# A delta-rule attention kernel: the first pair's blocks inverted in halves of 16 tokens, and the first loads dealt out over three queues

## The chip, the cores and the metric

The kernel runs on one core of a Trainium2 chip. The metric is the device time of one execution in microseconds (us), as a median of several runs. Beside it stands a profile: one execution recorded by the hardware, whose span runs from the first to the last instruction. Engines are named as in the profile: PE is TensorE (PEld its weight loads), DVE is VectorE, ACT is ScalarE, POOL is GpSimd, SP is SyncE, which here only issues transfers.

## What is computed

A delta-rule attention over 4 batch elements, 8 heads, 768 tokens and a head size of 48, and then a feed-forward block with a cosine gate.

```python
k_n = k / (np.linalg.norm(k, axis=-1, keepdims=True) + 1e-06)
state = np.zeros((B, H, D, D))
for t in range(S):
    kt, vt, bt = (k_n[:, :, t], v[:, :, t], beta[:, :, t, None])
    y[:, :, t] = np.einsum('bhd,bhde->bhe', q[:, :, t], state)
    v_old = np.einsum('bhde,bhd->bhe', state, kt)
    state = state + bt[:, :, :, None] * np.einsum('bhd,bhe->bhde', kt, vt - v_old)
# x is y as (3072, 384): batch and token by head and dimension
h = x @ w_in             # 384 -> 2048
out = (h * np.cos(h)) @ w_out    # 2048 -> 384
```

The kernel doesn't go token by token. It takes a unit of 32 tokens (of all 4 batch elements and 8 heads, 128 rows by 8 heads) at a time, 24 units, two of which form a pair. Within a unit the tokens depend on each other through a triangular 32x32 matrix for each head and batch element, one plus the scaled Gram matrix of the keys above the diagonal. That matrix is inverted, and the inverse is multiplied with the right side (the values less what the state already holds): this is called the solve. The state is then updated once for the unit. The feed-forward block works on pairs: eight hidden steps (products with w_in, then the gate) and an output (products with w_out).

The weights arrive as 64-bit floats and are turned into 32-bit ones on the chip, in 12 blocks of w_in and 16 of w_out, each by ACT, DVE and POOL one after the other.

## The kernel before

A small scheduler in the kernel file orders the work: every task is added with an engine, a cost, the tasks it depends on and a due time, and the instructions are written in the order that a simulation of the engines gives. Its constants are numbers found by tuning; they set the order and nothing else. Each engine then runs its own list strictly in order.

The loads at the start (each tensor of a unit is four transfers, one for each batch element):

```python
load(0, "k")                                   # on SP
near = 130 + C
for cols in (slice(0, near), slice(near, consts_np.shape[1])):
    nc.gpsimd.dma_start(out=consts[:, cols], in_=consts_dr.ap()[:, cols])
load(0, "q", nc.scalar)
for b in range(B):
    nc.gpsimd.dma_start(out=bq[...], in_=beta[b])
load(1, "q")                                   # on SP
load(1, "k", nc.gpsimd)
```

The Gram matrix of a unit is scaled by DVE into g (gram_keys) and written to DRAM (gram_put). Once both units of a pair are there, it is read back with one matrix to each partition row, the same to two partitions (gram_get), and inverted column by column. Each of the two partitions holds every second row of the inverse:

```python
def gram_get(m):
    g_dr = gbs[m]
    gbs[m] = work.tile([128, C, C], FP, name="gb", bufs=GBS)
    for a in range(SPLIT):                     # SPLIT = 2
        nc.sync.dma_start(out=gbs[m][half(a)]..., in_=g_dr...)

def invert(m, tag, columns):
    a, z = gbs[m], zs[m]
    eng = nc.gpsimd if tag is None else nc.vector
    for j in columns:                          # 0 .. C - 2, C = 32
        rows = j // SPLIT + 1
        shape = [128, rows, C - 1 - j]
        ...
        eng.tensor_tensor(                     # L583
            out=part,
            in0=z[:, 0:rows, j, None].to_broadcast(shape),
            in1=a[:, j, None, j + 1 :].to_broadcast(shape),
            op=ALU.mult,
        )
        behind = z[:, 0:rows, j + 1 :]
        eng.tensor_tensor(out=behind, in0=behind, in1=part, op=ALU.subtract)   # L590
```

Pair 0 is inverted by DVE, with z in PSUM (named p_i), and copied to SBUF by ACT (invert_out, L594). All later pairs are inverted by POOL with z in SBUF. The inverse goes to DRAM in one transfer (put, L599) and comes back with four transfers for each unit (get, L608), in the layout that the solve needs:

```python
def get(n):
    zts[n] = work.tile([128, H, C], FP, name="zt")
    z_dr = z_drs[n // 2].rearrange("r s u h b i -> u b (r s) h i")[n % 2]
    for b in range(B):
        nc.sync.dma_start(out=zts[n][quarter(b)], in_=z_dr[b])

def solve(n):
    zt, rhs = zts.pop(n), rhss.pop(n)
    p_u = p_us[n] = bank("one", [128, H, D], "p_u")
    for h in range(H):
        for b in range(B):                     # 32 products of 32x32 by 32x48; L652
            nc.tensor.matmul(p_u[quarter(b), h], zt[quarter(b), h], rhs[quarter(b), h])
```

A unit then goes: solve_out (u, DVE, L660), update (p_s, PE, L673), update_out (st, DVE), within (p_kq, PE, L690), within_out (y, ACT, L701), features (p_z, PE), features_out (x_ffn, ACT, L715), and its columns of x are ready. The first four hidden steps of pair 0 (L728) need only unit 0, the other four unit 1; step k of each four needs the first 3(k+1) blocks of w_in. Later pairs' hidden steps are L745, the outputs L792 and L850. Tiles of g have two buffers, those of u two.

Of the kernel before, what the change touches and what calls it, by code (L numbers as in the profile page):

```python
# [11 lines left out]
FP = mybir.dt.float32  # L12
# [5 lines left out]
C = 32  # L18
# [7 lines left out]
def _consts():  # L26

    p = np.arange(128)
    share = p // 64
    row = SPLIT * np.arange(C // SPLIT)[None, :] + share[:, None]
    return np.concatenate(
        [
            np.eye(128),
            p[:, None] % C < np.arange(C)[None, :],
            p[:, None] // C % 2 == np.arange(2)[None, :],  # L40
            (row[:, :, None] == np.arange(C)).reshape(128, -1),
        ],
        axis=1,
    ).astype(np.float32)


class Order:
# [9 lines left out]
    WINDOW = 133.06  # L57
    LAG = {"PE": 0.2, "DVE": 0.15, "ACT": 0.15, "POOL": 0.2, "SP": 2.0}
    IN_FLIGHT = 8
    STICK = 4.36  # L60
    CHANGE = 0.15
    SMALL = ("gram", "state", "solve", "update", "within")
# [4 lines left out]
        "turn": 16, "gram": 128, "state": 256, "solve": 128, "update": 64, "within": 128,  # L67
# [44 lines left out]
    def run(self, wrote):  # L112
# [8 lines left out]
        for key in ends:  # L121
            engine, cost, due, *_, moves = self.tasks[key]
            for d in self.tasks[key][4]:
# [3 lines left out]
                if left[d] == 0:  # L127
                    ends.append(d)
        for count, (key, task) in enumerate(self.tasks.items()):
# [97 lines left out]
def kernel(  # L227
# [44 lines left out]
    GBS, ZS = 2, 2  # L272
    GATES = 9
# [67 lines left out]
    near = 130 + C  # L341
    for cols in (slice(0, near), slice(near, consts_np.shape[1])):
        nc.gpsimd.dma_start(out=consts[:, cols], in_=consts_dr.ap()[:, cols])
# [3 lines left out]
    eye = consts[:, 130 + C :].rearrange("p (r i) -> p r i", i=C)  # L347
# [3 lines left out]
    for b in range(B):  # L351
        nc.gpsimd.dma_start(
            out=bq[C * b : C * b + H].rearrange("p n t -> p (n t)"), in_=beta[b]
        )
    load(1, "q")
    load(1, "k", nc.gpsimd)
# [165 lines left out]
    def gram_keys(n):  # L522
        g = gs[n] = work.tile([128, H, C], FP, name="g")
# [17 lines left out]
    def gram_put(n):  # L541
        m = n // 2
        if m not in gbs:
            gbs[m] = dram.tile([2, H, B, C, C], FP, name="g_dr")
        nc.sync.dma_start(
            out=gbs[m][n % 2].rearrange("h b j i -> (b j) h i"), in_=gs.pop(n)
        )

    def gram_get(m):

        g_dr = gbs[m]
        gbs[m] = work.tile([128, C, C], FP, name="gb", bufs=GBS)
        for a in range(SPLIT):
            nc.sync.dma_start(
                out=gbs[m][half(a)].rearrange("p j i -> p (j i)"),
                in_=g_dr.rearrange("u h b j i -> (u h b) (j i)"),
# [8 lines left out]

    def invert(m, tag, columns):

# [4 lines left out]
        eng = nc.gpsimd if tag is None else nc.vector  # L572
        for j in columns:
            rows = j // SPLIT + 1
            shape = [128, rows, C - 1 - j]
            if tag is None:
                part = work.tile([128, ROWS * C // 2], FP, name="part")
            else:
                part = ffn_pool.tile([128, ROWS * C // 2], FP, name="part_v", tag="o")
            part = part[:, 0 : shape[1] * shape[2]].rearrange(  # L580
                "p (r i) -> p r i", i=shape[2]
            )
            eng.tensor_tensor(  # L583
                out=part,
                in0=z[:, 0:rows, j, None].to_broadcast(shape),
                in1=a[:, j, None, j + 1 :].to_broadcast(shape),
                op=ALU.mult,
            )
            behind = z[:, 0:rows, j + 1 :]
# [13 lines left out]
    def get(n):  # L603

        zts[n] = work.tile([128, H, C], FP, name="zt")
        z_dr = z_drs[n // 2].rearrange("r s u h b i -> u b (r s) h i")[n % 2]
        for b in range(B):
            nc.sync.dma_start(out=zts[n][quarter(b)], in_=z_dr[b])  # L608
# [38 lines left out]
    def solve(n):  # L647
        zt, rhs = zts.pop(n), rhss.pop(n)
        p_u = p_us[n] = bank("one", [128, H, D], "p_u")
        for h in range(H):  # L650
            for b in range(B):
                nc.tensor.matmul(  # L652
                    p_u[quarter(b), h], zt[quarter(b), h], rhs[quarter(b), h]
                )

    def solve_out(n):

        u = us[n] = work.tile([128, H, 2, D], FP, name="u")
# [250 lines left out]
    def store(p, i, cols=slice(0, DM)):  # L909
# [10 lines left out]
            tt=LEAD + 1, g_gram=2, g_dr=3, gb=GBS, z=ZS, z_dr=3, zt=2, rhs=2, u=2, y=2,  # L920
            x=2, turns=2, r=2, g=GATES, o=2, o_out=2,
        ),
        free={"SP": 5.5, "ACT": 5.6, "POOL": 6.2, "DVE": 6.0, "PE": 6.0},
# [3 lines left out]
    W_IN, W_OUT, LOADS = 62.2, 33.46, -16.83  # L927
    PLAIN = range(1)
    outs_done = [None]
    START = 67.36  # L930
# [314 lines left out]
```

## Time and profile before

| what | us |
|---|---|
| time, median of 3 runs | 702.89 (701.24 to 702.93) |
| span of the profiled execution | 699.6 |
| PE busy | 639.3 (91%) |
| DVE busy | 402.9 (58%) |
| ACT busy | 283.2 (40%) |
| POOL busy | 342.5 (49%) |
| first matmul of a hidden step (p_h, L728) | at 68.45 |
| longest waits: POOL for gb from DRAM, over the whole run | 167.0, in 9 waits |

Times inside the profile count from the start of the span. A row of the groups has the line and engine, the operation, what is written and read, the count, then busy time and mean nanoseconds of one, then idle time of that engine just before it and what ended it. A row of the stretches (one row for each piece of the span that was asked for) has each engine's busy time with its number of instructions. "issue" in a chain of waits is time in which an engine waited for nothing that the profile shows. SPq, ACTq and POOLq are the engines' sequencers; a DMA instruction there is the issue of a transfer and not its duration. The time of an instruction on POOL is rough.

### The profile page before, as it was taken

The numbers are of one execution on the slowest core, as the hardware profiler recorded it, in microseconds if no ns is written. First come the engines' busy times: TensorE is split into PE (matmuls) and PEld (weight loads), VectorE is DVE, ScalarE is ACT, GpSimd is POOL, SyncE is SP. The second block draws the span as 40 slices with busy tenths as digits, with TensorE's granted clock in tenths as the row PEclk, the third lists the DMA queues.
The fourth block names the chain that finished last, engine by engine and source line by source line (L and its number), as shares of the span: only waits on it lengthen the run. The fifth ranks groups of instructions, "written<-read, shape, count | busy, mean of one in ns | idle before, by whom it ended". The sixth has DMA issues, their size and how long they took to land.

```text
span 699.6 us, 25291 instructions
## 1 busy us (share of the span) xinstructions
PE 639.3 (91%) x11096; PEld 568.9 (81%) x11096; DVE 402.9 (58%) x804; ACT 283.2 (40%) x482; POOL 342.5 (49%) x738
## 2 busy tenths in 40 slices
PE   3305799999999999999999999999999999999997
PEld 2205697777898988998998988998998988988997
DVE  4895778876655545556556555556456455444542
ACT  3424467652443542532533532532532532433430
POOL 5469678878508607708607707708508508500000
PEclk9999999999999999999999999999999999999999
DMA  9888656562323133133133133132122120110000
GB/s 174 195 173 181 131 144 162 131 121 38 63 54 72 28 73 72 27 74 70 30 72 72 29 70 72 30 73 48 22 57 49 22 58 26 22 22 14 1 23 22
DMA packets 162833, 49.27 MB, mean 70 GB/s; under 512 B 154212, under 2 KB 157428, under 8 KB 162724
## 3 DMA queue, kind: packets, MB, share of 16 engines
q1 hardware_dynamic: 161252, 46.82, 32.6%
q8 instruction: 87, 1.43, 0.9%
q0 software_dynamic: 384, 0.64, 0.4%
q10 hardware_dynamic: 1088, 0.20, 0.1%
q14 instruction: 22, 0.18, 0.1%
HBM read 36.62 MB, written 11.01 MB: 68 GB/s over the span
## 4 chain that ended last, share of the span: by engine, by line
PE 86%; DMA 5%; DVE 4%; issue 1%; ACT 1%; SPq 1%; ACTq 0%; POOL 0%; DVEq 0%
PE p_h L745 32%; PE p_out L850 29%; PE p_kq L625 4%; PE p_h L728 4%; PE p_s L673 3%; PE p_kq L690 3%; PE p_out L792 3%; PE p_u L652 3%; PE p_g L514 2%; PE p_t L496 2%; PE p_o L850 1%; SPq L330 1%; DVE p_i L590 1%; DVE part_v L583 1%; DMA kp<-in_k_dram 1%
## 5 line engine op out<-in xcount | busy, mean ns | idle before, releaser
L745 PE MATMUL p_h<-x_ffn,w_in 128*128 128x256 f32 x1056 | 241.7, 381 | 1.3 <-DVE g_ffn L782 1.3
L583 POOL TENSOR_TENSOR part<-z,gb 128x126 f32<-128x126 f32 (+22 forms) x341 | 131.2, 385 | 218.4 <-DMA gb<-g_dr 167.0
L745 PEld LDWEIGHTS p_h<-x_ffn,w_in 128*128 128x128 f32 x1056 | 197.1, 190 | 26.8 <-PE p_kq L625 1.0
L590 POOL TENSOR_TENSOR z<-z,part 128x126 f32<-128x126 f32 (+22 forms) x341 | 137.1, 402 | 26.7
L762 DVE SCALAR_TENSOR_TENSOR r<-p_h,turns 128x512 f32<-128x512 f32 x96 | 66.1, 689 | 114.9 <-ACT turns L758 113.7
L850 PE MATMUL p_out<-w_out,g_ffn 128*128 128x192 f32 x672 | 126.0, 333 | 0.8
L758 ACT ACTIVATE turns<-p_h 128x512 int32<-128x512 f32 x96 | 57.1, 594 | 167.6 <-PE p_h L745 154.2
L850 PEld LDWEIGHTS p_out<-w_out,g_ffn 128*128 128x128 f32 x672 | 108.7, 190 | 6.2 <-ACT o L887 3.0
L782 DVE TENSOR_TENSOR g_ffn<-r,p_h 128x512 f32<-128x512 f32 x96 | 65.5, 683 | 53.0 <-ACT r L770 52.7
L850 PE MATMUL p_out<-w_sum,g_ffn 128*128 128x192 f32 x496 | 89.7, 329 | 0.2 <-DVE o L900 0.2
L866 DVE TENSOR_TENSOR g_ffn<-g_ffn 128x256 f32<-128x256 f32 x176 | 79.2, 471 | 15.0 <-PE p_out L850 13.0
L769 ACT ACTIVATE r<-r 128x512 f32<-128x512 f32 x96 | 60.7, 632 | 62.0 <-DVE r L762 61.9
L850 PEld LDWEIGHTS p_out<-w_sum,g_ffn 128*128 128x128 f32 x496 | 81.7, 190 | 2.3 <-DVE o L900 0.4
L770 ACT ACTIVATE r<-r,halfpi 128x512 f32<-128x512 f32 x96 | 69.3, 722 | 3.1
L496 PE MATMUL p_t<-consts,kp 128*128 128x128 f32 x96 | 16.8, 305 | 41.2 <-DMA vp<-in_v_dram 29.6
L900 DVE SCALAR_TENSOR_TENSOR o<-p_out,o 128x192 f32<-128x192 f32 x74 | 25.4, 356 | 48.5 <-PE p_out L850 48.2
L496 PEld LDWEIGHTS p_t<-consts,kp 128*128 128x128 f32 x96 | 13.0, 157 | 43.8 <-issue 38.1
L701 ACT COPY y<-p_kq 128x384 f32<-128x384 f32 x24 | 11.5, 479 | 69.5 <-PE p_kq L690 69.5
L455 POOL TENSOR_TENSOR knrm<-ksum,halves 128x16 f32<-128x16 f32 (+1 forms) x14 | 36.5, 2613 | 5.9 <-DVE ksum L443 3.3
L625 PEld LDWEIGHTS p_kq<-st,kq_t 48*32 48x32 f32 x2944 | 29.4, 107 | 7.1 <-issue 7.0
L625 PE MATMUL p_kq<-st,kq_t 48*32 48x48 f32 x2944 | 32.8, 216 | 1.6 <-issue 1.6
L502 ACT COPY kq_t<-p_t 128x512 f32<-128x512 f32 x48 | 25.7, 588 | 15.9 <-PE p_t L496 15.9
(73 smaller groups left out, 619.8 us busy)
## 6 DMA issues: line engine op xcount, KB each, us to landing
pairs<-in_moe_w_in_dram SPq DMA_DIRECT2D x12, 512.0 KB
gb<-g_dr SPq DMA_DIRECT2D x24, 256.0 KB
pairs<-in_moe_w_out_dram SPq DMA_DIRECT2D x16, 384.0 KB
vp<-in_v_dram SPq DMA_DIRECT2D x96, 48.0 KB
kp<-in_k_dram SPq DMA_DIRECT2D x92, 48.0 KB
qp<-in_q_dram SPq DMA_DIRECT2D x92, 48.0 KB
out_dram<-o SPq DMA_DIRECT2D x23, 192.0 KB
g_dr<-g SPq DMA_DIRECT2D x24, 128.0 KB
```

Of the source, the lines that this page charges most:

```text
L496: nc.tensor.transpose(p_t[:, a, j], src[:, 2 * j : 2 * j + 2], ident)
L583: eng.tensor_tensor(out=part, in0=z[:, 0:rows, j, None].to_broadcast(shape), in1=a[:, j, None, j + 1 :].to_broadcast(shape), op=ALU.mult,)
L590: eng.tensor_tensor(out=behind, in0=behind, in1=part, op=ALU.subtract)
L625: nc.tensor.matmul(p_kq[quarter(b), par, a, j], kq_t[rows48(par), a, j, quarter(b)], st[rows48(par), b // 2, j, b % 2], start=(j == 0 and ...
L745: nc.tensor.matmul(p_h[:, i], w_in[:, t, (f + i) * 128 : (f + i + 1) * 128], xts[p][:, t], start=(t == 0), stop=(t == KT - 1),)
L758: nc.scalar.activation(turns[p, f], p_hs[p, f], AF.Copy, scale=TURN)
L762: nc.vector.scalar_tensor_tensor(out=r, in0=p_hs[p, f], scalar=TURN, in1=turns.pop((p, f)), op0=ALU.mult, op1=ALU.subtract,)
L769: nc.scalar.activation(r, r, AF.Abs)
L770: nc.scalar.activation(r, r, AF.Sin, bias=halfpi, scale=-2.0 * math.pi)
L782: nc.vector.tensor_tensor(out=out, in0=rests.pop((p, f)), in1=p_hs.pop((p, f)), op=ALU.mult,)
L850: nc.tensor.matmul(p_o, left(p, e // 2, a)[:, e % 2], right(e, b), start=(e == 0), stop=(e == FT // 2 - 1), skip_group_check=True,)
L866: nc.vector.tensor_tensor(out=left(p, k, to), in0=left(p, k, one), in1=left(p, k, two), op=op)
```

## The change

Three things are done at once, and the schedule's constants are set anew.

First, pair 0's matrices are inverted in halves of 16 tokens. Only the two 16x16 blocks on the diagonal are inverted, both in the same instructions (the access pattern gets one more dimension of two, from a block to the next), which leaves 15 columns. The 16x16 block between them is not inverted. It is used in the solve instead, for units 0 and 1: solve with the two small inverses, keep the first half's rows (half_out), multiply them with the Gram matrix (cross), take this from the right side of the second half (cross_out), and solve again. For this the tile g must stay in SBUF up to the cross product, so it has four buffers; u has one.

Second, the loads at the start. Unit 1's keys move from the POOL queue to SP, ahead of unit 1's queries. The second part of the constants (the unit matrix that z starts from) comes after beta.

Third, the two transfers of pair 0's gram_get are dealt to SP and ACT, and so are those of get for units 0 and 1.

The meaning is to have the first unit's result, and with it the first hidden step, earlier.

```diff
-    WINDOW = 133.06
+    WINDOW = 74.02
-    STICK = 4.36
+    STICK = 3.35
...
+    HALVED = range(1)
+    GRAMS = 4
...
-    for cols in (slice(0, near), slice(near, consts_np.shape[1])):
-        nc.gpsimd.dma_start(out=consts[:, cols], in_=consts_dr.ap()[:, cols])
+    nc.gpsimd.dma_start(out=consts[:, :near], in_=consts_dr.ap()[:, :near])
...
+    nc.gpsimd.dma_start(out=consts[:, near:], in_=consts_dr.ap()[:, near:])
+    load(1, "k")
     load(1, "q")
-    load(1, "k", nc.gpsimd)
...
+    def twice(ap, step):
+        dims = list(ap.ap)
+        return bass.AP(tensor=ap.tensor, offset=ap.offset, ap=dims[:1] + [(step, 2)] + dims[1:])
...
+        n = C // 2 if m in HALVED else C
         for j in columns:
             rows = j // SPLIT + 1
-            shape = [128, rows, C - 1 - j]
+            shape = [128, rows, n - 1 - j]
+            if n < C:
+                shape = [128, 2] + shape[1:]
...
+            column = z[:, 0:rows, j, None].to_broadcast([128, rows, n - 1 - j])
+            row = a[:, j, None, j + 1 : n].to_broadcast([128, rows, n - 1 - j])
+            behind = z[:, 0:rows, j + 1 : n]
...
+                column = twice(column, (ROWS // 2) * C + n)
+                row = twice(row, n * C + n)
+                behind = twice(behind, (ROWS // 2) * C + n)
+            eng.tensor_tensor(out=part, in0=column, in1=row, op=ALU.mult)
             eng.tensor_tensor(out=behind, in0=behind, in1=part, op=ALU.subtract)
...
+    def solve_half(n):
+        p_us[n] = bank("one", [128, H, D], "p_u")
+        quarters(p_us[n], zts[n], rhss[n])
+    def half_out(n):
+        v = us[n] = work.tile([128, H, D], FP, name="y")
+        nc.scalar.activation(v, p_us.pop(n), AF.Copy, scale=first_half)
+    def cross(n):
+        p_us[n] = bank("one", [128, H, D], "p_u")
+        quarters(p_us[n], gs.pop(n), us.pop(n))
+    def cross_out(n):
+        rhs = work.tile([128, H, D], FP, name="rhs")
+        nc.vector.scalar_tensor_tensor(
+            out=rhs, in0=p_us.pop(n), scalar=less_second, in1=rhss[n],
+            op0=ALU.mult, op1=ALU.add,
+        )
+        rhss[n] = rhs
...
-        u = us[n] = work.tile([128, H, 2, D], FP, name="u")
+        u = us[n] = work.tile([128, H, 2, D], FP, name="u", bufs=1)
...
-    W_IN, W_OUT, LOADS = 62.2, 33.46, -16.83
+    W_IN, W_OUT, LOADS = 57.76, 55.7, 4.07
-    START = 67.36
-    FIRST, STEP = 3.98, 5.5
+    START = 40.69
+    FIRST, STEP = 3.12, 5.9
...
+        if m == 0:
+            add(("gram_get", m), "SP", 0.6, lambda: gram_get(m, range(1)), puts, ...)
+            add(("gram_get2", m), "ACT", 0.6, lambda: gram_get(m, range(1, 2), nc.scalar), puts, ...)
...
+        if n < 2:
+            add(("get", n), "SP", 0.95, lambda: get(n, range(2)), [("put", m)], ...)
+            add(("get2", n), "ACT", 0.95, lambda: get(n, range(2, 4), nc.scalar), [("put", m)], ...)
...
-    add(("beta",), "DVE", 1.3, spread_beta)
+    there = []
+    for key, time in (
+        (("k", 0), 6.6), (("q", 0), 0.3), (("k", 1), 0.8), (("beta_there",), 0.9), (("q", 1), 0.6),
+    ):
+        add(key, "FIRST", time, lambda: None, there, due=0.0)
+        there = [key]
+    add(("beta",), "DVE", 1.3, spread_beta, [("beta_there",)])
```

START, FIRST and STEP set the due times of the hidden steps; W_IN, W_OUT and LOADS those of the weights' additions and loads; WINDOW how far ahead of the most urgent task an engine may go; STICK how long TensorE stays with tasks of one kind. The last part of the diff tells the schedule's simulation when the first loads are there; it emits nothing.

## The prediction

> **What bounds the kernel now.** I read the page's strip of 40 slices first, because this kernel has two regimes and an average over both says nothing. Its first row is TensorE, one digit for 17.5 us.
>
> ```profile
> PE   3305799999999999999999999999999999999997
> ...
> DMA  9888656562323133133133133132122120110000
> ```
>
> From the sixth slice on, TensorE is 9 of 10 in every slice; before that it is mostly idle. While it idles, the DMA row stands at 8 to 9. So the steady part is bound by TensorE and the start by something else. I then cut the span at the events that end each part of the start (the inversion's first and last VectorE instruction, the first solve, the first matmul of pair 0's hidden layer). Columns: stretch, its length, busy time and instructions of PE, PEld, DVE, ACT and POOL, granted clock, DMA share, GB/s.
>
> ```profile
> 0.00:29.36 29.36, 12.41 (x288) 10.11 (x288) 16.44 (x50) 12.58 (x23) 17.87 (x22) 1.00 0.91 187
> 29.36:47.47 18.11, 0.00 (x0) 0.00 (x0) 15.99 (x62) 4.95 (x8) 6.06 (x19) 1.00 0.80 170
> 47.47:58.90 11.43, 1.94 (x8) 1.57 (x9) 8.55 (x12) 2.15 (x4) 10.10 (x18) 1.00 0.78 163
> 58.90:68.45 9.55, 7.54 (x291) 6.46 (x292) 4.45 (x6) 4.69 (x10) 8.61 (x14) 1.00 0.90 211
> 68.45:97.00 28.55, 23.29 (x594) 21.52 (x590) 20.15 (x31) 14.78 (x29) 21.24 (x27) 0.94 0.67 141
> ```
>
> In the first 97 us TensorE works 45.2 us, so 51.8 us are lost there: 46.6 before the hidden layer starts at 68.45, 5.3 between 68.45 and 97. After 116.6 us, by the same view, it works 575.2 of 583.0. What the change can win must come from the start; in the rest only TensorE work counts.
>
> Next, the chain of waits over the start (start, us, what):
>
> ```profile
> 7.23 5.33 DMA kp<-in_k_dram
> ...
> 18.98 4.61 DMA g_dr<-g
> 23.61 0.55 SPq L554
> 24.21 5.06 DMA gb<-g_dr
> 29.59 0.21 DVE p_i L590
> ...
> 47.56 0.59 ACT z L594
> 48.17 0.39 SPq L599
> 48.61 3.39 SPq L330
> ```
>
> Keys, Gram matrix, a trip through DRAM, then 18.1 us in which one VectorE chain is alone on the path, then another trip through DRAM. On the way back the SP queue first issues other loads, with 3.39 us in one of them, before it comes to the inverse. Last, the groups by shape inside the inversion (mean ns is the third number from the end of a row's middle part):
>
> ```profile
> L590 DVE TENSOR_TENSOR p_i<-p_i,part_v 128x136 f32<-128x136 f32 x1 | 0.3, 307 | 0.0
> L583 DVE TENSOR_TENSOR part_v<-p_i,gb 128x136 f32<-128x136 f32 x1 | 0.3, 299 | 0.0
> ...
> L590 DVE TENSOR_TENSOR p_i<-p_i,part_v 128x16 f32<-128x16 f32 x1 | 0.2, 183 | 0.0
> L583 DVE TENSOR_TENSOR part_v<-p_i,gb 128x16 f32<-128x16 f32 x1 | 0.2, 175 | 0.0
> ```
>
> Eight and a half times the elements cost only 124 ns more. The number of instructions is what the inversion pays for.
>
> [...] 1.03 ns per element, and a fixed part of 158 to 166 ns. [...] the engines are busy 0.91 in the first 29 us, while four loads of one tensor take SP 1.8 to 1.9 us to issue. So I count issue time and no bandwidth. [...] In the trace the 64 small matmuls of a solve take 2.00 us at 58.93, after a pause, and 0.88 us at 75.24. I take those durations; the granted clock shown for that stretch is 1.00, so the trace shows the slowness and not its cause.
>
> **The change, part by part.**
>
> *Inversion.* Removed: 31 columns of two VectorE instructions. Left: 15 columns, each doing both 16-token halves in one instruction. From the rows above a column costs 158 + 166 + 2 x 1.03 ns per element, plus two gaps; 62 instructions sum to 16.0 us busy in 18.1 us, so a gap is 34 ns. A column is thus 392 ns + 2.06 ns per element. The old columns have 2856 elements: 31 x 0.392 + 5.88 = 18.0 us, against 18.11 measured, so the formula holds. The new ones have 744: 15 x 0.392 + 1.53 = 7.4 us. Saved: **10.7 us**, all of it on the path. [...]
>
> *Three-step solve of units 0 and 1.* Added per unit: two more batches of 64 matmuls, a ScalarE pass over 128x384 from PSUM (0.48 us for the same size at L701), a VectorE pass over 128x384 (0.56 at L640), and four handoffs of about 0.15 us (0.14 from u to p_s, 0.30 from p_u to u). [...] the first batch takes the place of today's 2.00 us, the two added are like L690's 1.50 us. Sum: 2 x 1.5 + 0.48 + 0.56 + 0.6 = **4.6 us added** on the path. Unit 1's extra latency lies beside pair 0's hidden matmuls, which need only unit 0 for their first half; its TensorE time is 2 x 0.88 = **1.8 us**, and it counts only if TensorE is full there, half of it by my guess: 0.9.
>
> *First loads.* Keys of unit 1 leave the POOL queue, where they come behind beta and the constants (issued 4.56 to 7.25, used at 12.33), for SP directly behind unit 0's keys. There they would be issued by about 5.3, where unit 1's queries are now. The first queries land 7.2 - 2.7 = 4.5 us after their last issue, so the keys are there by about 9.8, and the queries, moved back by 1.8 us, by about 11.6. Today ScalarE waits in order for the late keys (4.82 us at 12.33) and with it the copies of unit 0. I give this **2.5 us**. The Gram blocks read back over two queues: one issue less in a row, **0.6 us**.
>
> *The way back of the inverse.* 11.43 us pass between the last VectorE instruction and the first solve. With unit 0's reads over SP and ScalarE, two issues of 0.45 us drop out, and ScalarE's half need not stand behind SP's values loads. Of SP's 4.88 us there I give it **1.5 us** in all, because the SP half can still be late.
>
> Sum at the first hidden matmul: 10.7 + 2.5 + 0.6 + 1.5 - 4.6 = 10.7 us, so it comes at about 57.8 instead of 68.5. Less 0.9 for unit 1: a gain of about 9.8 us. The retuned constants of the schedule may recover some of the 5.3 idle us after 68.45; I add 0.7. That gives 702.9 - 10.5 = **692.4 us**, 1.5% less.
>
> **Rivals.** First, the weights become the wait. The first pair's hidden layer needs all twelve blocks of w_in. ScalarE waits 29.9 us in all for w_in before 68.45, the last block reaches it at 67.81, and the DMA engines are 0.86 busy up to there. For this: a start 10 us earlier asks for 6.3 MB earlier at an already high share. Against: only three blocks are needed for the first matmul and the last for the fourth, some 10 us later, and the DMA share is 0.78 to 0.80 between 29 and 59. It would leave half the gain: 697.
>
> Second, POOL becomes the bound. Its inversion of pair 1 starts at 40.0 (10.8 us of waiting for gb) and ends at 77.0, and eight w_in additions of 1.3 us come at 68.66 and later, the last ending near 92; the fourth hidden step starts only at 94.97. If pair 1's blocks do not reach POOL earlier, TensorE starts earlier and then starves, and the saturated stretch begins where it does now. For: that work isn't shortened at all. Against: POOL idles 28 to 40, the schedule's dues are set anew, and earlier Gram blocks start its inversion earlier. Taken alone it would leave 3 to 5 us: 698 to 700.
>
> Third, the loads and queues bring more than I gave, since the changed order puts the attention's loads ahead of the weights: if both trips through DRAM (4.6 and 5.1 us of landing in the first) fall to about 3 us, another 4 us come: 688. A last one: new waits in order, since ScalarE now has to stand for the block's landing before it issues its half, with w_in's conversion and the new half-solve pass on the same engine. That costs 2 to 4 us: 695 to 696.
>
> **Range and chances.** The arithmetic of the inversion is safe to about 1 us; the loads, the way back and POOL's supply are each good to 3 or 4 us, mostly independent. I take 685.5 to 699.5 for 8 in 10. Faster by over 2% needs less than 688.8, which asks for the third rival without the first two: 0.24. Slower by over 2% would need a steady state spoilt by the new constants, which TensorE at 575 of 583 us makes unlikely: 0.03. Within 2%: 0.73.
>
> **What would show it.** In the changed profile the 15 columns should take 7.4 us; the first solve, its pass, the cross product, its pass and the second solve 6 to 7 us from end to end; Gram blocks should be put near 16 us instead of 19; the first hidden matmul should stand near 58; TensorE should be full from about 87 instead of 97, and busy 3.5 us more in all. If the first hidden matmul is early but the strip fills at the same slice as now, the second rival is right; if ScalarE's wait for w_in moves to the gap between the hidden steps, the first. If the inversion is much longer than 7.4 us, or the first hidden matmul stays beyond 63, my chain is wrong.

## The result and the profile after

The change makes the kernel slower, by a little. The median goes from 702.43 us (4 runs, 701.24 to 702.93) to 705.83 us (4 runs, 704.48 to 706.35). The ratio is 1.0048, with a 95% interval of 1.0028 to 1.0068. In two later sets of runs, on two chips, the same kernel gave 1.0077 and 1.0065 (after_again and after_third, below). The prediction was 692.4.

The strip of 40 slices of the changed kernel, TensorE and DMA:

```profile
PE   4215989989999999999999999999999999999997
...
DMA  7886375453215134034035034024023030110000
```

TensorE now has a 9 in the fifth slice, where it had a 7, so its early work is denser. But the sixth slice (88 to 106 us) and the ninth (141 to 158) are 8 now, and were 9. In this profile, what was won at the left is lost again there. Cut at the same events as in the prediction (first and last instruction of the inversion, first solve, first hidden step), with one more stretch up to 150 us; the columns are those of the prediction's view:

```profile
0.00:30.59 30.59, 12.64 (x288) 9.85 (x288) 17.44 (x51) 13.28 (x24) 14.66 (x18) 1.00 0.81 178
30.59:37.99 7.40, 0.00 (x0) 0.00 (x0) 6.40 (x31) 1.20 (x2) 0.53 (x1) 1.00 0.83 188
37.99:57.00 19.01, 1.97 (x8) 1.58 (x9) 5.68 (x9) 4.16 (x7) 15.69 (x38) 1.00 0.79 160
57.00:71.37 14.37, 10.62 (x420) 9.11 (x420) 8.68 (x13) 7.13 (x14) 12.49 (x26) 1.00 0.62 180
71.37:97.00 25.63, 22.65 (x654) 21.12 (x655) 19.44 (x28) 12.78 (x24) 17.14 (x13) 1.00 0.47 107
97.00:150.00 53.00, 46.90 (x916) 38.42 (x916) 44.62 (x74) 34.30 (x64) 39.80 (x74) 1.00 0.56 136
```

Read the second number of each row, the length. The inversion fell from 18.1 to 7.4 us. It begins 1.2 us later than before, though, the stretch from its end to the first solve grew from 11.4 to 19.0 us, and the one from there to the first hidden step from 9.6 to 14.4. So the first hidden step comes at 71.37 us, 2.9 us later than before. One profile places such an event only to within some 4 us: b_adds (below) has the lists of the kernel before up to there, and its first hidden step is at 64.64 instead of 68.45. The changed kernel's three profiles have it at 71.00 to 71.37. What is certain is that none of the 10.7 us saved in the inversion arrives.

Why the way back grew is in SyncE's own list. It issued in order: from 62.3 to 69.2 us it stands for pair 1's inverse, and the weight block behind that goes out only at 69.64. Timeline of SyncE in the changed kernel (start, us, issuing line, what is loaded):

```profile
16.97 2.03 SPq L340 DMA_DIRECT2D qp<-in_q_dram  x4
...
19.61 3.63 SPq L557 DMA_DIRECT2D g_dr<-g  x3
...
40.30 1.93 SPq L340 DMA_DIRECT2D kp<-in_k_dram  x4
...
42.82 0.39 SPq L626 DMA_DIRECT2D z_dr<-z  x1
43.34 5.07 SPq L340 DMA_DIRECT2D qp<-in_q_dram  x4
...
51.88 1.85 SPq L636 DMA_DIRECT2D zt<-z_dr  x4
```

ScalarE has copied the inverse by 38.67, but SyncE writes it out (z_dr) only at 42.82: values, keys and weights stand ahead of it. Its half of the read back (zt) goes out at 51.88, 9 us later, behind queries that alone take 5.07 us to issue. ScalarE's half went out at 48.40. In the same way the Gram blocks of unit 0 were ready at 12.98 and those of unit 1 at 15.03 (15.86 and 18.96 before), but the first write (g_dr) is issued at 19.61, behind keys and queries of a later unit. Before the change it was issued at 18.27.

The solve in three steps, on TensorE:

```profile
57.02 1.77 PE L680 MATMUL p_u<-vp,zt 32*32 32x48 f32 x64 [5.33 <-issue]
59.45 1.50 PE L680 MATMUL p_u<-y,g 32*32 32x48 f32 x64 [0.67 <-ACT y L690]
61.70 1.65 PE L680 MATMUL p_u<-rhs,zt 32*32 32x48 f32 x64 [0.74 <-DVE rhs L698]
...
71.37 5.14 PE L781 MATMUL p_h<-x_ffn,w_in 128*128 128x128 f32 x24 [0.66 <-ACT x_ffn L768]
```

From the first batch to u, which VectorE begins at 63.41, it is 6.4 us, against 2.3 before. The profile's groups count the added matmuls (after, then before; behind the bar stand busy us and the mean ns of one):

```profile
L680 PE MATMUL p_u<-rhs,zt 32*32 32x48 f32 x1600 | 22.8, 205 | 0.7 <-DVE rhs L698 0.7
L680 PE MATMUL p_u<-y,g 32*32 32x48 f32 x128 | 2.4, 239 | 0.7 <-ACT y L690 0.7
```

```profile
L652 PE MATMUL p_u<-rhs,zt 32*32 32x48 f32 x1472 | 20.7, 203 | 0.1
```

With the first solve's own row (1.8 us after, 2.0 before) that is 27.0 against 22.7: 4.3 us more for 256 matmuls. TensorE's busy time in all rose by 3.2 (639.3 to 642.5) and its idle time by 1.0 (60.3 to 61.3), which makes the 4.2 us of the span (699.6 to 703.8). In the other two profiles of the changed kernel the busy time is 3.6 and 4.4 us above that before, and the idle time 1.2 and 0.4 below. So the idle time, which the change was meant to cut, stayed about what it was.

TensorE's busy time by stage, from the view by stretches (from 150 to 690 us it works 538 to 539 of 540 us in both kernels, so the race is over there):

| kernel | 0 to 60 | 60 to 97 | 97 to 150 |
|---|---|---|---|
| before | 15.4 | 29.8 | 51.0 |
| after | 16.9 | 31.0 | 46.9 |
| after_again (the same kernel) | 17.3 | 30.2 | 49.8 |
| after_third (the same kernel) | 17.1 | 31.7 | 47.4 |

Up to 97 us the changed kernel is ahead by 2.3 to 3.6 us of work, between 97 and 150 it falls behind by 1.2 to 4.1. What delays that stage begins at 60. SyncE's list again, in the changed kernel:

```profile
58.98 3.32 SPq L340 DMA_DIRECT2D kp<-in_k_dram  x4
69.16 0.39 SPq L626 DMA_DIRECT2D z_dr<-z  x1
...
80.55 0.38 SPq L557 DMA_DIRECT2D g_dr<-g  x1
...
84.35 0.40 SPq L415 DMA_DIRECT2D pairs<-in_moe_w_out_dram  x1
...
95.76 0.40 SPq L557 DMA_DIRECT2D g_dr<-g  x1
```

It stands from 62.3 to 69.2 for pair 1's inverse, which GpSimd is still making, and from 70.9 to 80.6 for unit 4's Gram blocks. So the second w_out block is asked for only at 84.35. VectorE then stands 3.28 us for its split, the state of unit 1 comes late behind that, unit 5's Gram matrix (90.68 on TensorE, 84.63 before) behind the state, and its write at 95.76 (85.98 before). GpSimd gets pair 2's blocks at 106.83 instead of 98.23:

```profile
106.83 0.24 POOL L616 TENSOR_TENSOR part<-z,gb 128x31 f32<-128x31 f32 x1 [6.41 <-DMA gb<-g_dr]
```

The bracket says that GpSimd was idle for 6.41 us before it, for this transfer. What follows in its list is late as well: the first w_out addition behind this inversion's end began at 141.34 before and begins at 149.06 now.

The profile's chain of waits names the path that ended last. In the kernel before, it comes from pair 0's inversion and goes over unit 0 to the first hidden step (start, us, what):

```profile
62.32 1.56 PE p_s L673 x32
...
68.52 0.94 PE p_h L728 x3
```

In the changed kernel it doesn't touch unit 0's solve or the first hidden step:

```profile
34.27 3.98 DMA gb<-g_dr
...
67.22 0.61 POOL z L617
69.08 2.91 POOL knrm L467
72.02 1.25 DVE knrm L478
...
83.37 1.02 POOL w_out L438
```

It comes from pair 1's Gram blocks (gb) and goes through the whole of pair 1's inversion on GpSimd. The change does not shorten that inversion, which began at 38.41 instead of 40.00. Then the chain goes through pair 2's norms and scales, which unit 4's Gram blocks need, for which SyncE stands until 80.6. The other two profiles of this kernel show the same chain up to there. So unit 0's path was no longer the one that ended last.

### The profile page after: what moved, and what is told of

It is laid out like the page before. It is cut to its first block, busy times and chain, and to the rows that moved or that the text cites. A ratio compares the mean times of both kernels' runs of the same rounds, so it can differ in the third digit from the quotient of the medians.

```text
span 703.8 us, 25771 instructions
## 1 busy us (share of the span) xinstructions
PE 642.5 (91%) x11352; PEld 571.1 (81%) x11352; DVE 396.6 (56%) x774; ACT 283.1 (40%) x484; POOL 340.1 (48%) x734
## 3 DMA queue, kind: packets, MB, share of 16 engines
q1 hardware_dynamic: 161172, 46.63, 31.7%
## 4 chain that ended last, share of the span: by engine, by line
PE 78%; POOL 7%; DMA 6%; SPq 3%; issue 2%; DVE 2%; ACT 1%; ACTq 0%; POOLq 0%
PE p_h L798 32%; PE p_out L903 28%; PE p_kq L653 3%; POOL part L616 3%; POOL z L617 3%; PE p_kq L743 2%; PE p_u L680 2%; PE p_s L726 2%; SPq L340 2%; PE p_t L508 2%; PE p_out L845 2%; PE p_g L526 2%; DMA kp<-in_k_dram 1%; PE p_o L903 1%; DMA gb<-g_dr 1%
## 5 line engine op out<-in xcount | busy, mean ns | idle before, releaser
L903 PE MATMUL p_out<-w_sum,g_ffn 128*128 128x192 f32 x496 | 87.8, 326 | 0.0
L508 PE MATMUL p_t<-consts,kp 128*128 128x128 f32 x96 | 16.9, 306 | 31.9 <-DMA qp<-in_q_dram 22.9
L429 DVE SCALAR_TENSOR_TENSOR pairs<-pairs 128x384 uint32<-128x384 uint32 (+1 forms) x28 | 22.4, 800 | 22.5 <-ACT pairs L425 22.5
```

Source lines behind the costliest of these rows:

```text
L508: nc.tensor.transpose(p_t[:, a, j], src[:, 2 * j : 2 * j + 2], ident)
L903: nc.tensor.matmul(p_o, left(p, e // 2, a)[:, e % 2], right(e, b), start=(e == 0), stop=(e == FT // 2 - 1), skip_group_check=True,)
```

## The experiments

The theories were these. A: the inverse's trip stands behind other loads in SyncE's list. B: the three-step solve loses more than the halving wins. C: the new constants, which put every list in another order, lose. D: the rate of the loads bounds the start. E: GpSimd is the second bound, since only four w_in blocks are added before it has inverted pair 1. F: the time between 97 and 150 us decides; in the later runs F is the jam in SyncE's list just shown. L, W and S are explained where they come. In the kernels named as moves, each engine keeps its own list of tasks but for the moves given; "w7" is the load of weight block 7, counted from 0, of which 0 to 11 are w_in; put, get and gram_get are the trips through DRAM; k5 is a load of unit 5's keys; split, shift and add are the steps of a weight block on ScalarE, VectorE and GpSimd; square and sum belong to the norms of the keys; inv(1,i) is a stretch of pair 1's inversion.

All ratios are to the kernel before, run on the same chip.

| run | ratio | 95% interval | first hidden step at |
|---|---|---|---|
| e_no_cross | 1.0089 | 1.0058 to 1.0119 | 67.60 |
| e_sp_first | 1.0112 | 1.0076 to 1.0147 | 70.69 |
| e_chain_first | 1.0104 | 1.0068 to 1.0140 | 59.89 |
| e_chain_pool | 1.0130 | 1.0106 to 1.0155 | 61.88 |
| c_full | 1.0043 | 1.0027 to 1.0058 | 68.94 |
| c_halves_alone | 1.0090 | 1.0068 to 1.0111 | 71.03 |
| c_old_numbers | 1.0048 | 1.0034 to 1.0062 | 65.86 |
| c_loads_alone | 1.0149 | 1.0126 to 1.0172 | 66.76 |
| after_again | 1.0077 | 1.0052 to 1.0102 | |
| after_third | 1.0065 | 1.0044 to 1.0085 | 71.10 |
| f_flow | 1.0048 | 1.0034 to 1.0061 | 70.31 |
| f_flow_chain | 1.0058 | 1.0037 to 1.0079 | 58.92 |
| b_adds | 1.0029 | 1.0016 to 1.0042 | 64.64 |
| g_free_pool | 1.0032 | 1.0017 to 1.0047 | 62.09 |
| g_free_pool_alone | 1.0058 | 1.0034 to 1.0082 | 70.71 |
| d_weights | 1.0083 | 1.0050 to 1.0115 | 62.13 |
| b_thrice | 1.0102 | 1.0076 to 1.0127 | 72.89 |

**The start of the chain.** e_no_cross keeps the changed kernel's lists, but the half solve and the cross product emit nothing: it leaves out the block between the two halves, with its 256 matmuls.

```diff
-        p_us[n] = bank("one", [128, H, D], "p_u")
-        quarters(p_us[n], zts[n], rhss[n])     # and half_out, cross, cross_out
+        pass
```

> Every engine's list as in the changed kernel, but the half solve, its pass, the cross product and its pass write nothing (units 0 and 1 use only the two small inverses: the block between them is left out of the result). Theory A (the inverse's trip through DRAM stands behind other loads in SP's list, and the three-step solve costs TensorE time): TensorE works 4 to 5 us less, and the time falls by 3 to 5 us, to 701 to 703. Theory B (the three-step solve alone is what made the change lose): it falls by 10 or more, to 696 or less. Theory C (the new order loses late): it falls by less than 2 us.

The first hidden step came 3.8 us earlier, as it must, and the ratio (1.0089) is no lower than that of the change. So the time of the three-step solve is not what the end waits for in this order, and theory B falls. The chain of waits agrees: it goes again through pair 1's inversion on GpSimd, from Gram blocks at 33.14 to the norms at 68.35, and not through unit 0's solve.

e_sp_first takes theory A at its word:

```diff
  SyncE:
- ... q4 v1 k5 w6 put(0) q5 v2 w7 get(0) get(1) ...
+ ... v1 w6 put(0) get(0) get(1) q4 k5 q5 v2 w7 ...
  ScalarE: get2(0) and get2(1) ahead of square(2,0), the squares of pair 2's keys
```

> Order alone: on SP unit 1's values and block 6 of w_in, then the inverse's write and the reads for units 0 and 1, all ahead of the loads of units 4 and 5; on ScalarE its half of the reads ahead of the squares of pair 2. Theory A: the inverse is issued at 39 to 40 us instead of 42.8, the first solve starts 5 to 8 us earlier (49 to 52), the first hidden matmul follows by 4 to 8 us, and the time falls by 3 to 6 us, to 700 to 703. Theory D (the DMA engines' rate bounds the start, so order doesn't matter): w_in's blocks come later by what the others come earlier, the first hidden matmul moves by less than 2 us, the time stays within 1.5 us of 705.8.

The first hidden step moved by 0.7 us only, since unit 0's tasks also had others ahead of them on ScalarE and VectorE. The ratio was 1.0112.

e_chain_first moves these too (its first moves are those of e_sp_first):

```diff
  ScalarE: split(6), half_out(0), within_out(0), features_out(0) ahead of square(2,0); turn_out(4) ahead of split(7)
  VectorE: gram_queries(2), shift(6), cross_out(0), solve_out(0), update_out(0) ahead of sum(2,0); right(1) ahead of weigh(1)
  TensorE: turn(4) ahead of hidden(0,0)
```

> As e_sp_first, and on TensorE, VectorE and ScalarE the tasks of unit 0 from the half solve to x ahead of those of unit 4 and of blocks 6 and later of w_in. Theory A: first hidden matmul at 57 to 61 us; but POOL still has its eight w_in additions behind pair 1's inversion, so the second hidden step stays near 76 to 79 us and the time falls by 3 to 7 us only, to 699 to 703. Theory D: as before, within 1.5 us of 705.8.

Now the way back is short: the inverse is written at 37.40, read from 42.67, the first solve is at 44.65, and the first hidden step at 59.89, 8.6 us ahead of the kernel before. So theory A is right about the first hidden step and wrong about the end, which came no earlier (1.0104). TensorE's timeline shows what follows that step:

```profile
59.89 3.02 PE L781 MATMUL p_h<-x_ffn,w_in 128*128 128x128 f32 x24
...
71.03 0.80 PE L781 MATMUL p_h<-x_ffn,w_in 128*128 128x128 f32 x2
...
73.42 4.35 PE L781 MATMUL p_h<-x_ffn,w_in 128*128 128x128 f32 x20 [0.44 <-POOL w_in L438]
```

The second step starts at 71.03 and waits in it for w_in additions of GpSimd, which come right after pair 1's inversion. This spoke for theory E.

e_chain_pool moves additions of w_in in among pair 1's inversion:

```diff
  GpSimd: add(4), add(5) ahead of inv(1,2); add(6) ahead of inv(1,4); add(7), add(8) ahead of inv(1,6)
```

> As e_chain_first, and on POOL the additions of w_in's blocks 4 to 8 between the pieces of pair 1's inversion instead of behind it. Theory E (POOL holds the second bound: only four blocks of w_in are ready until pair 1 is inverted, so hidden steps 2 to 4 can't start before 71, whenever the first does): second hidden step at 62 to 66 us instead of 71 to 73, and the time falls by 3 to 6 us against e_chain_first, to a ratio of 0.996 to 1.006. Theory F (the later part of the start, 97 to 150 us, is set by w_out and the outputs): second step early, time within 2 us of e_chain_first.

It is worse. GpSimd waited only 1.0 us for the blocks, but with five additions in front of its end pair 1's inverse was written at 76.85 instead of 67.88, and the second hidden step still came at 73.51.

**Parts of the change alone.** c_full undoes the halving in the changed kernel; c_halves_alone keeps the halving and takes back loads, queues and constants; c_old_numbers takes back the constants alone; c_loads_alone takes back halving and constants and keeps the loads and queues, but also the buffers of the changed kernel (four of g, one of u).

```diff
 c_full, c_loads_alone
-    HALVED = range(1)
+    HALVED = range(0)
 c_halves_alone, c_old_numbers, c_loads_alone
-    WINDOW = 74.02        # and STICK, W_IN, W_OUT, LOADS, START, FIRST, STEP
+    WINDOW = 133.06
```

> The changed kernel with the halving undone alone (31 columns, one solve); loads, two queues and the constants stay, and the order is worked out anew. Theory A: the loads that now stand behind the inversion are hidden by it again, TensorE works 3 us less, and the time is 702 to 706. Theory C (the new constants and loads lose): like the changed kernel, 705 to 708. If the halving had gained its 10.7 us on the path it would be 712 or more.

> The kernel before with the halving and the three-step solve alone: loads, queues and constants are those of before. Theory E: the first hidden step comes 2 to 8 us earlier, but the second stays at 75 to 79 us, and the time is 1 to 4 us above the kernel before (ratio 1.001 to 1.006), since TensorE has 3 us more to do. Theory C (the new constants lose what the halving wins): 5 us or more below the kernel before, ratio 0.993 or less.

> The changed kernel with the schedule's constants (WINDOW, STICK, W_IN, W_OUT, LOADS, START, FIRST, STEP) of the kernel before. Theory C: ratio 0.993 or less. Theory E: 1.000 to 1.008, as in the changed kernel, since POOL's list still has pair 1's inversion ahead of the additions.

> The kernel before with only the first loads dealt over three queues and the two-queue reads of pair 0's Gram blocks and inverse; its own scheduler constants and the full inversion stay. Theory C (it is the new constants and the order that come from them which lose): 1.000, within 0.002. Theory L (the dealt loads put the first weights and later loads back and lose by themselves): 1.003 or more. If the loads work as they were meant to, 0.997.

> The changed kernel once more, as a measure beside the other runs of this set. Every theory: a ratio to the kernel before of 1.003 to 1.010.

Set side by side: with the constants of before, the loads alone cost 1.49%, the halving alone 0.90%, and both together 0.48%. With the new constants the loads cost 0.43% without the halving and 0.48 to 0.77% with it. Effects that don't add, and a combination better than either part, mean that no part has a price of its own. Each of these kernels has another set of lists; that the lists decide is the likely reading, not one that a run isolates. In c_loads_alone, the worst, TensorE works 44.3 us between 97 and 150 (51.0 before), although its first hidden step is 1.7 us earlier than in the kernel before. Theory C fails as far as it blames the new constants alone: with the old ones and the same parts (c_old_numbers) a loss of 0.48% stays.

**The jam.** f_flow changes only SyncE's list in the changed kernel:

```diff
+ k7 ahead of put(1); w13 and w14 ahead of gram_put(4); w15 ahead of q6
+ gram_put(5) and gram_get(2) ahead of v4
```

> The changed kernel with only SyncE's list changed between 59 and 110 us: key load 7 goes in front of the way out of pair 1's inverse, the loads of the second and third w_out blocks in front of the way out of unit 4's Gram blocks, and the way out of unit 5's Gram blocks and pair 2's Gram read in front of a value and a query load. Theory F (the end is set by a jam in SyncE's list: between 62 and 84 us it stands for pair 1's inverse and unit 4's Gram, the second w_out block is issued at 84.4, VectorE stands for it, unit 5's Gram and so pair 2's inverse start 8.6 us later than before the change): the second w_out block is issued near 76, pair 2's inverse starts near 99 instead of 106.8, the last w_out addition of the first 16 ends by 145 instead of 150, TensorE's idle time between 97 and 150 us falls from 6.1 to about 3, and the ratio to the kernel before falls from 1.0077 to about 1.003. Theory E (GpSimd's work is the bound until 83 us and sets the rest): the ratio stays within 0.002 of 1.0077.

The lists did what was asked: unit 5's Gram blocks are written at 89.37 instead of 95.76, and GpSimd begins pair 2 at 96.86:

```profile
96.86 0.24 POOL L616 TENSOR_TENSOR part<-z,gb 128x31 f32<-128x31 f32 x1
```

TensorE's idle time from 97 to 150 was 4.6 us (expected about 3), within the 3.2 to 6.1 of the changed kernel's own three profiles. The ratio of 1.0048 is below the changed kernel's 1.0077 and 1.0065, but equal to its first, and the intervals overlap: pair 2's inversion starts 10 us earlier, and a gain at the end is not shown.

f_flow_chain adds all moves of e_chain_first to f_flow.

> The same together with the edits that brought the first hidden step to 59.9 us (unit 0's chain first on every engine). Theory F: with both jams out of the way the early start reaches the end, 4 us or more below the changed kernel, ratio at or below 1.001. Theory E: the four w_in blocks that are ready before pair 1's inversion ends near 69 us still limit TensorE to one hidden step before 71 us, so the chain's gain is lost again and the ratio is that of the SyncE cure alone, within 0.002.

1.0058: with both jams cured, an early start (58.92) still brings nothing. The view by stretches (0 to 60, 60 to 97, 97 to 150):

```profile
0.00:60.00 60.00, 23.98 (x720) 19.72 (x721) 31.68 (x92) 20.30 (x37) 34.50 (x64) 1.00 0.78 168
60.00:97.00 37.00, 26.89 (x657) 24.11 (x657) 27.39 (x42) 21.18 (x38) 27.20 (x30) 0.82 0.63 153
97.00:150.00 53.00, 48.60 (x918) 40.22 (x918) 42.04 (x74) 33.32 (x62) 42.52 (x76) 0.97 0.55 133
```

Against the kernel before, TensorE does 8.6 us more in the first stretch, 2.9 less in the second and 2.4 less in the third. What is left, 3.3 us, is less than the 4.3 us of added matmuls. Nor need all of it be work done: in the changed kernel the 64 matmuls of a solve took 1.77 us at 57.02, after 5.33 us of idle time, and 0.88 at 76.44, right behind others, and the clock granted in f_flow_chain's second stretch was 0.82, against 1.00 in the first.

**Is GpSimd the second bound?** g_free_pool is f_flow_chain with pair 1's inversion left out from the fifth column on, so units 2 and 3 compute with another inverse. g_free_pool_alone does the same in the changed kernel's own order. b_adds asks it of the kernel before, by order alone.

```diff
-        for j in columns:
+        for j in columns if m != 1 or columns[0] < 4 else ():
```

```diff
  b_adds, in the kernel before
  GpSimd: add(7), add(8) ahead of add(12)
  TensorE: hidden(0,4) ahead of update(1)
  ScalarE, VectorE: turns, rest, cos and gate of (0,4) ahead of split(14) and shift(14)
```

> The kernel with SyncE's list cured and unit 0's chain first, but pair 1's inversion on GpSimd leaves out all columns from the fifth on, so units 2 and 3 get another inverse (the output is not the reference's). Theory E: with GpSimd free from about 45 us the w_in additions follow their data, the second hidden step comes at 62 to 67 instead of 71.9 and the fourth before 80, and the time falls by 5 us or more against the same kernel with the inversion (1.0058), to below 0.999. Theory W (the end is set by the sum of TensorE's work and by w_out and the outputs' VectorE work after 97 us): within 0.003 of 1.0058.

> The changed kernel in its own order, with the same part of pair 1's inversion left out (the output is not the reference's). Theory E: first hidden step still at 71, the next three follow at once, ratio 1.000 or below against 1.0077 for the changed kernel. Theory W: within 0.003 of 1.0077.

> The kernel before with only its lists changed: GpSimd adds w_in blocks 8 and 9 (counted from 1) ahead of the first w_out block, TensorE does the third hidden step ahead of unit 1's state update, and the third step's work on ScalarE and VectorE goes ahead of the third w_out block's. Theory E (which of GpSimd's additions are done sets TensorE's filling): the third hidden step moves from 89.2 us to 82 to 85, TensorE's idle time between 77 and 97 us falls by 2 to 4 us, and the ratio is 0.995 to 0.998. Theory F (the end is set by SyncE's jam and pair 2's Gram): unit 5's Gram comes 2 to 3 us later behind the hidden step, and the ratio is 1.000 to 1.004.

Theory E falls as the one cause. With some 23 us of work taken from GpSimd (busy 317.8 us instead of 340.9) the ratio goes from 1.0058 to 1.0032 in one pair and from 1.0077 or 1.0065 to 1.0058 in the other: 2 us at most, with intervals that overlap, where 5 or more were expected. In g_free_pool_alone the chain of waits goes over unit 0 again, with its solve at 55.87 and the first hidden step at 70.71. So in the changed kernel two paths are tied: with GpSimd's taken away, unit 0's ends last, and hardly earlier. In g_free_pool the second hidden step still comes at 74.35, and GpSimd is idle for 20.95 us before its norms. What TensorE waits for now is the w_in blocks. VectorE's timeline there shows the shift of a block before and during GpSimd's additions:

```profile
64.55 0.69 DVE L429 SCALAR_TENSOR_TENSOR pairs<-pairs 128x512 uint32<-128x512 uint32 x1 [1.72 <-ACT pairs L425]
...
70.94 1.77 DVE L429 SCALAR_TENSOR_TENSOR pairs<-pairs 128x512 uint32<-128x512 uint32 x1
```

The last five w_in blocks were asked for between 57 and 63 us, and are split and shifted one after the other from 63 to 79. b_adds brought the third hidden step from 89.22 to 77.37 and the ratio to 1.0029, so even in the kernel before an earlier third step made the end no earlier.

d_weights is f_flow_chain with the w_in blocks brought forward on all four engines:

```diff
  SyncE:   w7, w8 ahead of q4; w9 ahead of v2; w10 ahead of v3; w12 ahead of put(1)
  ScalarE: split(7), split(8) ahead of within_out(0)
  VectorE: shift(7) ahead of update_out(0), shift(8) ahead of sum(2,0)
  GpSimd:  add(4), add(5), add(6) ahead of inv(1,5); add(7), add(8) ahead of inv(1,6)
```

> The kernel with SyncE's list cured and unit 0's chain first, and now the w_in blocks too: blocks 8 to 11 go ahead of query, key and value loads of pairs 1 and 2 on SyncE, blocks 8 and 9 are split and shifted on ScalarE and VectorE ahead of unit 0's state, and five additions of w_in go ahead of the last two stretches of pair 1's inversion on GpSimd. Theory D (after the chain the next bound is the arrival of the w_in blocks, which sit in the same list as the loads the chain needs): the second hidden step comes at 62 to 66 us instead of 71.9, the third before 75, and the ratio falls to 0.997 to 1.002 from 1.0058. Theory W (what the start gains is lost again, because TensorE then waits longer for w_out and pair 2 between 97 and 150 us and carries the added products): within 0.003 of 1.0058, with more idle time of TensorE after 77 us than in the kernel before.

1.0083: theory D fails in this form as well, and W holds as to where the time goes: TensorE's idle time after 77 us is larger than before the change (12.8 us of the 73 up to 150, against 5.4). The second hidden step stayed at 71.35. Then TensorE stands still for 7.86 us before unit 5's turn: the profile names no releaser. In the order of the tasks that turn follows unit 4's Gram, and that the scales from pair 2's norms, which GpSimd did at 75.07, after the inversion that the additions had pushed back. This last link is argued from the order, not measured.

**A later start.** b_thrice adds one suspected cost to the kernel before: units 0 and 1 do their solve's 64 matmuls three times into the same bank. after_third is the changed kernel on the same chip.

```diff
-        for h in range(H):
+        for h in [x for _ in range(3 if n < 2 else 1) for x in range(H)]:
```

> The kernel before, its lists unchanged, but units 0 and 1 do their solve's 64 matmuls three times into the same bank: the matmuls of the three-step solve without its copies and without the halving, 256 more in all. Theory W (TensorE's added work reaches the end one for one): by the first solve's durations in the kernel before (2.0 and 0.9 us) 5 to 6 us more on the way to the first hidden steps; at a share of 0.6 or more that arrives at the end, ratio 1.0045 to 1.008. Theory S (the start has slack, since 60 us of it are idle, and only its waits count): ratio within 0.002 of 1.

> The changed kernel as it is, on the same chip as the run above, so that the two can be set side by side. Both theories: 1.005 to 1.008, as before.

The 256 matmuls alone, with nothing won against them, cost 1.02%, some 7 us (interval 0.76 to 1.27%), at or above what theory W allowed and no less than the whole change on that chip (0.65%). Unit 0's solve, from its first matmul to u, took 6.15 us instead of 2.30, and pair 2's inversion came at 104.89 instead of 98.23. The chain of waits goes through this solve. Theory S falls: where a path ends last, it has no slack towards later.

## Why the prediction was wrong

**The inversion** was right: 15 columns took 7.40 us (30.59 to 37.99), 7.4 were predicted.

**The three-step solve** was right: 4.1 us added from the first batch to u against 4.6. TensorE's busy time rose by 3.2 against 3.5.

**First loads** failed. 2.5 us were to come from earlier keys. The Gram blocks were indeed ready sooner, by 2.9 us in unit 0 and 3.9 in unit 1, but their write was put at 19.61 and not near 16, since other loads stood ahead of it on SyncE. The term was worth nothing: the inversion began 1.2 us later than before. That dealing the loads out saves issue time and no bandwidth was the author's estimate, from DMA engines that were 0.91 busy in the first 29 us; no run shows it by itself. The 0.6 us of the two reads of the Gram blocks were won (issued at 25.07 and 25.11, beside each other) and are lost in the same delay.

**The inverse's way back** failed, and with the wrong sign: 1.5 us were to be won, 7.6 were lost. The prediction had seen the queue's 4.88 us ahead of the inverse and did not ask what an inverse that comes 10 us earlier meets in that list. It meets other loads: those that before were issued while VectorE was inverting. The prediction also took 1.8 to 1.9 us for the issue of four loads, where SyncE took up to 4.88 in the kernel before (at 48.61).

So the first hidden step stood at 71.37 and not at 57.8: 10.7 us won in the inversion, less 1.2 before it, 7.6 on the way back and 4.8 from the first solve on. Beyond 63, the prediction said, its chain would be wrong. But the step that carries the error is the next one: **"a gain of about 9.8 us" was passed from the first hidden step to the end, one for one.** e_chain_first and f_flow_chain cured the way back and put that step at 59.89 and 58.92, within about 2 us of the prediction, and were still slower than before. What the runs show in its place is that TensorE's early work is bounded by several paths that end at about the same time: the chain of unit 0, pair 1's inversion on GpSimd with pair 2's norms behind it, and the w_in blocks (loads, ScalarE, VectorE, GpSimd in a row). In the changed kernel the second of these ends last by the chain of waits. Shortening one of them gained 2 us at most; lengthening the one that ended last, in b_thrice, cost in full. The second rival had named GpSimd. Its sign, an early step with the strip filling no earlier than before, was seen in e_chain_first (TensorE's row begins 4237789999), and its mechanism stands in the chain of waits of the changed kernel. It was not the one bound, though, since unit 0's path ends hardly earlier.

**The constants** were to recover 0.7 us of idle time between the first hidden step and 97 us. It did fall, from 5.3 to 3.0 us, but no run shows that the constants did it. Between 97 and 150, where the prediction had counted on TensorE's work alone, 1.2 to 4.1 us were lost. The last rival, a new wait of ScalarE of 2 to 4 us, did not come: ScalarE issued its reads of the inverse at 48.40, 0.4 us after its instruction before.

What stays open: whether any order with the halved inversion beats the kernel before. None of the 17 runs did, 13 of which have it. Closest came g_free_pool (1.0032), with unit 0's chain first and pair 1's inversion cut short, where TensorE waits for the w_in blocks; all three paths were not shortened at once. The chain of waits explains why e_no_cross gains nothing over the changed kernel, but not all of its loss of 0.9% against the kernel before, which has as many matmuls.

## What to carry to other kernels

Before a saving on a critical chain is passed on to the end, list what else must arrive by the time that the chain would end, and move the chain alone in an experiment; in a kernel whose order was tuned, several paths can be tied, as here, and the chain is only one of them. The chain of waits of the changed kernel names the next one. A result that came earlier was worth nothing here while it stood behind other loads: the inverse, copied by 38.67 us, was written at 42.82, and SyncE's half of it was read only from 51.88. So go through the list of every engine that it passes, the DMA-issuing one first. And where a scheduler draws up the lists, any change redraws them all: here parts of one change gave ratios from 1.004 to 1.015 that did not add up, a spread nearly as large as the 1.5% that the change was meant to bring.

## What the runs showed of the hardware

Small VectorE instructions ran at GpSimd's pace while GpSimd added w_in blocks back to back. The scaling from pair 2's norms after the change, during eight additions of 1.3 us each, and the same in the kernel before, where two such additions had just ended and the inversion's shorter instructions followed:

```profile
73.29 1.21 DVE L480 TENSOR_TENSOR krec<-knrm 128x16 f32<-128x16 f32 x1
74.54 0.25 DVE L481 RECIPROCAL krec<-krec 128x16 f32<-128x16 f32 x1
```

```profile
72.20 0.18 DVE L468 TENSOR_TENSOR krec<-knrm 128x16 f32<-128x16 f32 x1
72.41 0.25 DVE L469 RECIPROCAL krec<-krec 128x16 f32<-128x16 f32 x1
```

An instruction of 0.18 us takes 1.21; the reciprocal behind it, with one input, takes 0.25 in both kernels. The four others of this scaling take 0.91 to 1.24 us each in the changed kernel, about one addition. The first of the five, TENSOR_SCALAR with one tensor as input, takes 1.24 us at 72.02 against 0.32 before, so the number of inputs alone does not tell which are slowed. The kernel before shows the same where an addition runs: the last of the five (bz), for the next pair, took 0.96 us at 101.14, beside a w_out addition of 1.01 us at 101.04, and 0.19 us at 73.08. No run shows the cause. The five instructions take from 72.02 to 76.99 in the changed kernel and from 71.84 to 73.27 in the one before: 3.5 us more, in front of unit 4's Gram blocks, while eight w_in additions run on GpSimd (71.95 to 82.61).

Issuing had no fixed cost either: four loads of one tensor took SyncE 1.93 us at 40.30 and 5.07 at 43.34, in the changed kernel.
